# Stacked low-rank product, turned queries, reused conversion buffers and another cost model for the order of the lead, in a one-core attention and mixer kernel

## Chip, cores and metric

The kernel runs on one core of a Trainium2 chip. The metric is the device time of one execution in microseconds (us). Three runs of the kernel before took 1488.79, 1486.19 and 1491.61 us, median 1488.79.

## The reference

Everything is float32. Eight batches (B), eight heads of 64, 576 positions (S), d_model 512.

```python
def sm_attn(qq, kk, vv):
    s = scale * np.matmul(qq, kk.transpose(0, 1, 3, 2))
    s = s - np.max(s, axis=-1, keepdims=True)
    a = np.exp(s)
    a = a / (np.sum(a, axis=-1, keepdims=True) + 1e-09)
    return np.matmul(a, vv)
p_packed = sm_attn(p, k, v)                # p: 32 packed queries per head
x = sm_attn(q, p_packed, p_packed)         # then heads side by side: [B, S, 512]

xk = mu_k * x + (1.0 - mu_k) * x_prev      # x_prev: x one position earlier
xr = mu_r * x + (1.0 - mu_r) * x_prev
k = np.maximum(xk @ w_k, 0.0)              # 512 -> 1024
x = sigmoid(xr @ w_r) * (k * k @ w_v)      # 1024 -> 512

h = x.transpose(0, 2, 1) @ U @ V           # over positions, rank 32
u = x + h.transpose(0, 2, 1)
out = u + np.maximum(u @ w_ch1, 0.0) @ w_ch2   # 512 -> 2048 -> 512
```

## The kernel before

**Parts.** The work falls into three stretches that follow each other on TensorE (PE).

- *The lead* does attention units 0 to 7. A unit is two batches and two heads; there are 16. `attention_steps` transposes K, P, the exponentials and Q with PE (`plan.transpose`, a matmul with the identity, tile `psat`), copies each result out of PSUM, and writes the unit's output `xo` to the DRAM tensor `x_d`. Units 0 to 7 are "plain" (`NPLAIN`), on four buffer sets; units 8 to 15 have a second form of the last softmax, all on buffer set A0.
- *Phase 1* walks 12 chunks of 384 rows (`chunks`, index `n`): mix with the previous position (`mix`), the sigmoid branch (`r_block`, `psr`), the hidden layer (`k_block`, `psk`), its output (`v_block`, `psv`), the product of both to the DRAM tensor `x2_d` (`x2_out`), and the low-rank sum over positions (`xu_block`, `psu`) to `xu_d`. Units 8 to 15 lie between its chunks 2 to 5.
- *Phase 2* has nine blocks `q` of four row tiles T (36 tiles of 128 rows). For each T, `load_u` reads the rows back, `h_block` multiplies by V and adds (`psh`), `t_block` transposes, `operands` makes the seven combinations of a Strassen step, and the loop over `f` (8 steps) does `product` (`psc`, 128x256) and `c2_block` (`psc`, 128x512) with the converted weights.

Float32 products are three float32r matmuls of a high and a low part (`split`: `hi` is a copy, `lo` a difference). The weights come as float64; `Cast.run` turns them into float32 with ACT and DVE operations on staging tiles (`cv.st`, three of 4 KB a row; `cv.tp`, tags "a" and "m", two each of 2 KB). From chunk 2 on, `casts` does V and the 32 tiles of `w_ch1` and `w_ch2` as background work, five a chunk, taking one tile of each weight in turn; `make_ws` builds the Strassen weights from `w_ch1` in chunks 10 and 11 and stores them in `ws_d`, from where GpSimd's queue fetches them all through phase 2 (`load_ws`).

**Queries of units 8 to 15.** `load_q` brings a unit's 288 KB with two DMAs, in runs of 64 floats, one unit ahead of their use (`claim`, `early`). Nine PE transposes of 128x128 in three groups, each followed by a copy (ACT or DVE, whichever the scheduler picks), make `qt`.

**The low-rank product.** `make_v` keeps V as a high and a low part, each with a zero half so that two batches share a tile; `load_xu` makes one tile `X` for two batches, the high part of U's product in one half of the partitions and the rest in the other. `h_block` runs two matmuls of 128x512 per T, one per part of V.

**The order.** Nothing is issued as written. `Plan` records every operation with its engine (or a choice of ACT and DVE), its class `cls` (lower goes first; casts and `make_ws` have 3) and what it depends on, and `emit` builds five queues (PE, ACT, DVE, GpSimd, SP) by simulating itself: each engine has a clock, an operation becomes ready at the end of what it needs plus a lag `LAT` between engines (127 ns from DVE to DVE), and takes a modelled duration; DMAs have modelled issue, transfer and landing times. Each queue then runs strictly in that order, SP's DMAs included: an entry that waits holds all behind it.

Of the kernel before, what the change touches and what calls it, by code (L numbers as in the profile page):

```python
# [9 lines left out]
F32 = mybir.dt.float32  # L10
# [90 lines left out]
class Plan:  # L101
# [234 lines left out]
    TICK = 10240.0 / 3.0  # L336

# [3 lines left out]
    def emit(self):  # L341
# [67 lines left out]
        while True:  # L409
# [46 lines left out]
            if op.cost == "dma":  # L456
                clock[e] = t + (60.0 if e == "sp" else 1000.0)
                dge = max(dge, t + 60.0) + 500.0
                wire = max(wire, dge + 700.0) + dur
                op.fin = wire + 1700.0  # L460
            else:
# [9 lines left out]
                clock[e] = t + dur  # L471
# [6 lines left out]
def packed_attention_moe_mixer_kernel(  # L478
# [98 lines left out]
    class Bufs:  # L577
# [24 lines left out]
        def tile_in(self, tag):  # L602
            return plan.tile(self.big_p, [P, 1152], F32, "big", parts=(0, 1, 2, 3), name=tag)
# [17 lines left out]
        def load_q(self, u, after=()):  # L621
# [3 lines left out]
            t = self.qin[u]  # L625
            for b2 in range(2):
# [21 lines left out]
    def attention_steps(A, u, u_next):  # L648
# [69 lines left out]
        for c in range(3):  # L718
            yield
            ps = ps_att()  # L720
            for t in range(3):
                i = 3 * c + t
                plan.transpose(ps[:, t * P:(t + 1) * P], qin[:, i * P:(i + 1) * P], ident)
            n = 3 if c < 2 or not plain else 2
            w = 8 if plain else NI
            plan.copy(
                qt[:, 0:w * P].rearrange("p (b i c) -> p i b c", b=2, i=w)[:, 3 * c:3 * c + n],
                ps[:, 0:n * P].rearrange("p (i c b) -> p i b c", i=n, b=2))
            if c == 2 and plain:
# [194 lines left out]
    es_w1, es_att, es_x, es_st = ExitStack(), ExitStack(), ExitStack(), ExitStack()  # L924
# [7 lines left out]
    cv = Cast(es_att, "right")  # L932
# [221 lines left out]
    vx_p, st_p, u_p, wb_p, w2r_p, tr_p = rpools = [Pool(bufs=n) for n in (1, 5, 4, 11, 1, 3)]  # L1154

    def open_r():
        es_att.close()
        for n, pl in zip("vx st2 u wb w2r tr".split(), rpools):
# [12 lines left out]
    c2_tags = [(home[t], t) for t in ["wk2_1", "wk3_1"] + [f"wv{m}" for m in range(MK)]]  # L1171
    c2_tags += [(w2r_p, "c2_0"), (w2r_p, "c2_1"), (xs_p, "xs")]
# [17 lines left out]
    def make_v():  # L1190
        vst = plan.tile(vx_p, [P, 2, NI, 2, 64], F32R, "vst", parts=(0, 1))
        vst_.append(vst)
        for c in range(2):
# [3 lines left out]
            for i0, i1 in ((0, 5), (5, NI)):  # L1197
                s = plan.tile(st_p, [P, 512], F32, "s", name="s_v")
                sv = s[:, 0:(i1 - i0) * 64].rearrange("p (i b c) -> p i b c", b=2, c=32)
# [367 lines left out]
```

## Time and profile before

The profiled execution took 1491.34 us; its span, from the first to the last instruction, is 1489.6 us, with 1.7 us around it. It is 2.55 us above the median of the three runs.

| what | in the profiled execution |
|---|---|
| span | 1489.6 us, 25587 instructions |
| PE, matmuls | 1461.4 us busy, 98% |
| DVE | 980.2 us, 66% |
| ACT | 728.3 us, 49% |
| GpSimd | 270.3 us, 18% |
| mean granted PE clock | 0.983 of 2.4 GHz |
| DMA | 292.42 MB, 196 GB/s over the span |

An engine's busy time is the sum of its instructions' spans. Matmuls overlap in the records (each is shown from its start to its modelled end), so the time that a run of matmuls really takes is read from the chain of waits or from start to start. "PEclk" is the granted clock, 1.00 for 2.4 GHz and 0.50 for 1.2 GHz; a value between them is a mean of a stretch that had both.

### The profile page before, as it was taken

Reading aid. Unit: us, or ns where it says so; the run is one execution under the profiler, and the core shown is the slowest. Engines: PE = TensorE matmul, PEld = TensorE weight load, DVE = VectorE, ACT = ScalarE, POOL = GpSimd, SP = SyncE. Lnnn points to the kernel's source line nnn. Section 1 sums busy time; section 2 is a strip of 40 time slices with the busy share of each in tenths; the row PEclk is TensorE's granted clock in tenths of the full one; section 3 lists DMA queues with packets and bytes.
Section 4 is the critical chain, followed back from the end, with each engine's and each line's share of the span. In section 5 each row is a group of like instructions: output and inputs, shape, how many; then the busy total and the mean of one; then the engine's idle time right before and its main releaser. Section 6 shows DMA issues by size and latency. Waiting matters only on the chain.

```text
span 1489.6 us, 25587 instructions
## 1 busy us (share of the span) xinstructions
PE 1461.4 (98%) x9208; PEld 1277.7 (86%) x9208; DVE 980.2 (66%) x2143; ACT 728.3 (49%) x1534; POOL 270.3 (18%) x522
## 2 busy tenths in 40 slices
PE   6999999999999999999999999999999999999998
PEld 5667888888888888889899999899999999999997
DVE  6677877788888888786855464545555555554533
ACT  5567656666666666676533233323333332333332
POOL 0000000000000000001333333333333333333331
PEclk9689999999999999999999999999999999999999
DMA  8863335654655446666988888888888878878763
GB/s 233 234 175 121 114 101 137 205 182 136 186 179 156 141 141 218 207 226 191 314 228 237 211 208 245 198 244 229 231 212 229 213 201 239 213 216 222 206 176 99
DMA packets 213708, 292.42 MB, mean 196 GB/s; under 512 B 70224, under 2 KB 105360, under 8 KB 213584
## 3 DMA queue, kind: packets, MB, share of 16 engines
q1 hardware_dynamic: 141008, 158.65, 34.7%
q0 software_dynamic: 72576, 132.15, 34.0%
q8 instruction: 74, 1.21, 0.3%
q14 instruction: 50, 0.41, 0.1%
HBM read 229.84 MB, written 60.89 MB: 195 GB/s over the span
## 4 chain that ended last, share of the span: by engine, by line
PE 92%; DMA 3%; DVE 2%; SPq 1%; ACT 1%; issue 1%; DVEq 0%
PE psc L197 50%; PE psk L197 13%; PE psv L197 12%; PE psr L197 7%; PE psat L197 5%; PE psat L209 3%; SPq L319 1%; PE psh L197 1%; PE psu L197 1%; DMA kin<-in_k_dram 1%; DMA s<-w_d 1%; DMA qin<-in_q_dram 0%; DMA x_d<-xo 0%; DMA prs<-x_d 0%; DVE ob L254 0%
## 5 line engine op out<-in xcount | busy, mean ns | idle before, releaser
L197 PE MATMUL psc<-w,hid 128*128 128x512 f32 x1728 | 420.7, 391 | 0.2 <-ACT xu L288 0.2
L197 PEld LDWEIGHTS psc<-ob,wb 128*128 128x128 f32 x3024 | 386.4, 191 | 15.1 <-ACT tmp L288 0.8
L197 PE MATMUL psc<-ob,wb 128*128 128x256 f32 x3024 | 391.1, 282 | 0.4 <-ACT tmp L288 0.4
L319 POOL DMA_DIRECT2D wb<-ws_d x504 | 267.3, 530 | 565.5 <-PE psc L197 436.9
L197 PEld LDWEIGHTS psc<-w,hid 128*128 128x128 f32 x1728 | 314.9, 188 | 60.7 <-DVE hid L273 0.7
L233 ACT ACTIVATE hid<-tmp 128x256 fp32r<-128x256 f32 x216 | 131.6, 676 | 229.8 <-DVE tmp L254 229.8
L197 PE MATMUL psk<-xk,wk 128*128 128x384 f32 x1056 | 208.4, 340 | 1.3 <-ACT sq L233 0.8
L197 PE MATMUL psv<-wv,kk 128*128 128x512 f32 x783 | 202.0, 395 | 0.0
L197 PEld LDWEIGHTS psk<-xk,wk 128*128 128x128 f32 x1056 | 184.6, 188 | 10.6 <-issue 1.5
L197 PEld LDWEIGHTS psv<-wv,kk 128*128 128x128 f32 x783 | 144.2, 188 | 28.3 <-issue 0.8
L273 DVE SCALAR_TENSOR_TENSOR hid<-tmp,hid 128x256 fp32r<-128x256 f32 x216 | 126.5, 631 | 49.8 <-ACT hid L233 48.3
L254 DVE TENSOR_TENSOR tmp<-tmp,psc 128x256 f32<-128x256 f32 x288 | 113.1, 410 | 64.4 <-PE psc L197 64.1
L273 DVE SCALAR_TENSOR_TENSOR hid<-psc,hid 128x256 fp32r<-128x256 f32 x72 | 45.3, 629 | 166.5 <-ACT hid L233 166.5
L233 ACT ACTIVATE hid<-psc 128x256 fp32r<-128x256 f32 x72 | 45.9, 637 | 147.9 <-PE psc L197 147.5
L197 PE MATMUL psr<-wr,xr 128*128 128x512 f32 x414 | 112.3, 404 | 0.1
L311 POOL MEMSET x<- 128x8 f32 x4 | 0.5, 113 | 538.4 <-DVE m L270 538.1
L197 PEld LDWEIGHTS psr<-wr,xr 128*128 128x128 f32 x414 | 75.8, 190 | 18.4 <-issue 3.2
L288 ACT ACTIVATE tmp<-psc 128x256 f32<-128x256 f32 x144 | 56.5, 392 | 54.1 <-PE psc L197 53.5
L233 ACT ACTIVATE sq<-psk 128x384 f32<-128x384 f32 x96 | 46.5, 490 | 66.0 <-PE psk L197 63.6
L254 DVE TENSOR_TENSOR kk<-sq,kk 128x384 fp32r<-128x384 f32 x87 | 47.8, 552 | 32.0 <-ACT kk L288 31.8
L270 DVE SCALAR_TENSOR_TENSOR m<-x,mu_t,m 128x384 f32<-128x384 f32 x88 | 51.6, 610 | 0.9 <-ACT m L233 0.9
L233 ACT ACTIVATE m<-x,om_t 128x384 f32<-128x384 f32 x88 | 50.8, 607 | 2.5 <-DVE xr L254 1.8
(176 smaller groups left out, 1645.9 us busy)
## 6 DMA issues: line engine op xcount, KB each, us to landing
wb<-ws_d POOLq DMA_DIRECT2D x504, 256.0 KB, 3.7
st<-in_moe_w_ch_dram SPq DMA_DIRECT2D x32, 512.0 KB, 5.3
ws_d<-wb SPq DMA_DIRECT2D x56, 256.0 KB, 3.0
qin<-in_q_dram SPq DMA_DIRECT2D x32, 288.0 KB, 5.7
x_d<-xo SPq DMA_DIRECT2D x16, 576.0 KB, 3.4
x_d<-x SPq DMA_DIRECT2D x36, 256.0 KB, 2.2
u<-x_d SPq DMA_DIRECT2D x36, 256.0 KB, 5.2
out_dram<-u SPq DMA_DIRECT2D x36, 256.0 KB, 3.2
```

The costliest lines, as they stand in the source:

```text
L197: self.nc.tensor.matmul(o, l, r, start=start, stop=stop, **k)
L209: self.nc.tensor.transpose(out.get(), in_.get(), ident.get())
L233: self.nc.scalar.activation(o, in_.get(), func, **k)
L254: return self.elem(engs, lambda e, o, x, y: e.tensor_tensor(out=o, in0=x, in1=y, op=op), out, [a, b], self.TT, cls)
L270: ("dve",), lambda e, o, x, y, z: e.scalar_tensor_tensor(out=o, in0=x, scalar=z, in1=y, op0=op0, op1=op1), out, [a, b, s], {"dve": (1.042, ...
L273: ("dve",), lambda e, o, x, y: e.scalar_tensor_tensor(out=o, in0=x, scalar=s, in1=y, op0=op0, op1=op1), out, [a, b], self.TT, cls)
L288: self.nc.scalar.activation(o, i, AF.Copy)
L311: (self.nc.gpsimd if eng == "pool" else self.nc.vector).memset(o, 0.0)
L319: (self.nc.sync if eng == "sp" else self.nc.gpsimd).dma_start(out=o, in_=i)
```

## The change

Six things change.

1. **Turned queries.** For units 8 to 15 the nine PE transposes and their three copies go. `load_q` now brings Q with eight DMAs of 32 partitions in runs of 32 floats, arranged so that two 32x32-block transposes on DVE (`plan.turn`, 128x576 each) make `qt`.
2. **Stacked low-rank product.** V is kept as 12 slots of 64 columns, high part in two of the four 32-partition groups and low part in the other two, and `load_xu` makes one tile per batch (`X0`, `X1`) with the matching stack of four. One matmul then holds all four products for two row groups of one batch. A tile T is now two half tiles of one batch (`halves_of`), apart from the ninth of each batch pair, which still takes two matmuls. `load_u` and the output store use two DMAs of 64 rows for such a T.
3. **Buffers.** The staging pools of `Cast` stay open to the end (`es_cv`). In phase 2 the three `cv.st` tiles hold converted `w_ch2` tiles, and `cv.tp` holds `u` tiles; the pools `u` and `w2r` go, and `st2` has 6 buffers instead of 5.
4. **When conversions happen.** All of `w_ch1` is converted ahead of `w_ch2`; the phase-2 pools open after chunk 6, and `make_ws` runs two pairs a chunk in chunks 7 to 10 instead of four in chunks 10 and 11.
5. **Loads in the first block of phase 2.** `load_w2` and the `u` loads of the next block are tied to the step before (`after=(step,)`).
6. **The scheduler's model.** Below 150 us of modelled time (`AHEAD`) an operation of ACT or DVE that depends on one of the same engine is ready 100 or 83 ns before that one's end, not after a lag, and the engine's clock moves on that much earlier. From 500 us of modelled time (`CHUNKS`) DMAs have slower modelled figures. No instruction changes by this, only the order and the choice of ACT or DVE.

```diff
+    AHEAD = 150000.0
+    CHUNKS = 500000.0
+    OVER = {"act": 100.0, "dve": 83.0}
+    LEAD = (60.0, 500.0, 1.0, 1700.0)
+    LOADED = (300.0, 100.0, 1.19, 3000.0)
...
-                return max([p.fin + self.lag(p.eng, e) for p in op.preds], default=0.0)
+                return max([p.fin + (-self.OVER[e] if p.eng == e and e in self.OVER and p.fin < self.AHEAD
+                                     else self.lag(p.eng, e)) for p in op.preds], default=0.0)
...
-                clock[e] = t + dur
+                clock[e] = t + (max(dur - self.OVER.get(e, 0.0), 0.0) if t < self.AHEAD else dur)
...
+            if u >= NPLAIN:
+                for b2 in range(2):
+                    for h in range(2):
+                        src = q[2 * bp + b2, 2 * j + h].rearrange("(r t) (e s) -> e r t s", t=2 * NI, e=2)
+                        for e in range(2):
+                            g = 2 * h + e
+                            plan.dma(t.at(2 * g + b2)[g * 32:(g + 1) * 32, b2 * S:(b2 + 1) * S]
+                                     .rearrange("p (t s) -> p t s", s=32), src[e], after=after)
+                return
...
-        for c in range(3):
+        for c in range(3 if plain else 0):
...
+        if not plain:
+            yield
+            for b2 in range(2):
+                r = slice(b2 * S, (b2 + 1) * S)
+                plan.turn(qt[:, r].rearrange("p (i r e) -> p e i r", i=NI, e=2), qin[:, r])
...
-    vx_p, st_p, u_p, wb_p, w2r_p, tr_p = rpools = [Pool(bufs=n) for n in (1, 5, 4, 11, 1, 3)]
+    vx_p, st_p, wb_p, tr_p = rpools = [Pool(bufs=n) for n in (1, 6, 11, 3)]
...
+    c2_tags = [(cv.st, "st")] * 3
+    c2_tags += [(home[t], t) for t in ["wk2_1", "wk3_1"] + [f"wv{m}" for m in range(MK)]]
...
+        for b2 in range(2):
+            xa = plan.tile(st_p, [P, 512], F32, "s", parts=(0, 1, 2, 3), name="xa")
+            xb = plan.tile(st_p, [P, 512], F32, "s", parts=(0, 1, 2, 3), name="xb")
+            for g in range(4):
+                for a, t in ((0, xa), (1, xb)):
+                    r = a * 64 + b2 * NP
+                    plan.dma(t.at(g)[g * 32:(g + 1) * 32, :], xu_d[b][r:r + NP, :])
+            plan.tt(xa, xa, xb, add)
+            X = plan.tile(vx_p, [P, 512], F32R, f"X{b2}")
...
-        for a in range(2):
-            plan.mm(ps, vst_[0].at(a)[:, a, i].rearrange("p b c -> p (b c)"), xt[b], start=(a == 0), stop=(a == 1))
+        if t < NI - 1:
+            k2 = t % 4
+            plan.mm(ps, vst_[0][:, 2 * k2:2 * k2 + 2].rearrange("p e c -> p (e c)"), xt[b, t // 4],
+                    start=True, stop=True)
+        else:
+            for b2 in range(2):
+                plan.mm(ps, vst_[0][:, NI - 1 + 2 * b2:NI + 1 + 2 * b2].rearrange("p e c -> p (e c)"), xt[b, b2],
+                        start=(b2 == 0), stop=(b2 == 1))
...
-            if n == NCAST:
-                opened_r = plan.open(rpools, A0.pools + cv.pools, open_r)
-        if n > NCAST:
+        if n == FIRST_WS - 1:
+            opened_r = plan.open(rpools, A0.pools, open_r)
+        if FIRST_WS <= n < FIRST_WS + 4:
             plan.cls = 3
-            for f in range(NF // 2):
-                make_ws((n - NCAST - 1) * (NF // 2) + f)
+            for f in range(2):
+                make_ws(2 * (n - FIRST_WS) + f)
...
-                        load_w2(m)
+                        load_w2(m, (step,) if f else ())
```

`FIRST_WS` is 7 and `NCAST` stays 9. Three places show what the scheduler makes of it.

PE in phase 1 where unit 13 stands, before: three groups of three transposes of `qin` lie between the sigmoid branch's matmuls.

```order
L197 MATMUL psr<-wr_200,xr 128x512 x3
L209 MATMUL psat<-ident,qin 128x128 x3
L197 MATMUL psr<-wr_201,xr 128x512 x2
L209 MATMUL psat<-ident,qin 128x128 x3
L197 MATMUL psr<-wr_201,xr 128x512
L197 MATMUL psr<-wr_202,xr 128x512
L209 MATMUL psat<-ident,qin 128x128 x3
L197 MATMUL psr<-wr_202,xr 128x512
```

Now PE has none there, and DVE has two turns per unit, a low half of the hidden layer (`kk`) between them (the same unit).

```order
L254 TENSOR_TENSOR th<-qt,th 128x576
L215 STREAM_TRANSPOSE qt<-qin 128x2x288
L254 TENSOR_TENSOR kk<-sq,kk 128x384
L215 STREAM_TRANSPOSE qt<-qin 128x2x288
L254 TENSOR_TENSOR xr<-m,xr 128x384
```

So the work moved from PE, and from the copies behind it, to DVE's queue; SP's queue has the unit's Q as eight entries in a row where it had two.

PE in phase 2, a step of block 1, before: two matmuls of `psh` per T between the products.

```order
L197 MATMUL psc_9281<-ob,wb 128x256 x6
L197 MATMUL psh<-X,vst 128x512 x2
L197 MATMUL psc_9390<-ob,wb 128x256 x6
```

Now one, at a later step of the same block.

```order
L197 MATMUL psc_9352<-ob,wb 128x256 x6
L197 MATMUL psh<-X_9376,vst 128x512
L197 MATMUL psc_9472<-ob,wb 128x256 x6
```

Over the program `psh` has 72 matmuls before and 40 now; the ninth T of a batch pair keeps two.

PE in the lead, units 0 and 1 (`a_150` are unit 0's exponentials), before:

```order
L209 MATMUL psat<-ident,qin 128x128 x9
L209 MATMUL psat<-ident,kin 128x128 x8
L209 MATMUL psat<-ident,kin 64x128 x2
L209 MATMUL psat<-ident,pbd 128x128
L209 MATMUL psat<-ident,a_150 128x128 x5
L197 MATMUL psat<-kh,pT 32x256 x8
L197 MATMUL psat<-vin,at 32x64 x20
```

Now:

```order
L209 MATMUL psat<-ident,qin 128x128 x9
L209 MATMUL psat<-ident,a_150 128x128 x4
L209 MATMUL psat<-ident,kin 128x128 x4
L209 MATMUL psat<-ident,a_150 128x128
L209 MATMUL psat<-ident,kin 128x128 x4
L209 MATMUL psat<-ident,kin 64x128 x2
L209 MATMUL psat<-ident,pbd 128x128
L197 MATMUL psat<-kh,pT 32x256 x8
L197 MATMUL psat<-vin,at 32x64 x20
```

The same matmuls stand there, with unit 0's ahead of unit 1's; the order differs like this all through the lead, while SP's first 36 rows are the same and later ones change places by a few.

## Rows read from the trace of the kernel before

**Rows 1.** Page, part 1: busy time of each engine and its share.

```profile
PE 1461.4 (98%) x9208; PEld 1277.7 (86%) x9208; DVE 980.2 (66%) x2143; ACT 728.3 (49%) x1534; POOL 270.3 (18%) x522
```

**Rows 2.** Windows: stretch, length, busy us of each engine, PEclk, DMA share, GB/s.

```profile
0.00:60.00 60.00, 45.99 (x403) 34.91 (x404) 39.99 (x108) 31.56 (x89) 1.32 (x11) 0.80 0.84 234
60.00:146.00 86.00, 79.30 (x655) 56.24 (x654) 62.86 (x153) 59.28 (x158) 0.00 (x0) 0.86 0.54 160
...
220.00:510.00 290.00, 288.12 (x1984) 244.36 (x1983) 240.72 (x536) 198.35 (x427) 0.11 (x1) 1.00 0.55 166
...
706.00:728.00 22.00, 21.43 (x128) 18.41 (x127) 20.00 (x39) 13.53 (x28) 6.89 (x13) 1.00 0.95 294
728.00:1480.00 752.00, 752.00 (x4689) 679.87 (x4688) 401.65 (x835) 250.25 (x478) 254.44 (x480) 1.00 0.81 217
```

**Rows 3.** Page, part 4: the chain that ended last, by engine.

```profile
PE 92%; DMA 3%; DVE 2%; SPq 1%; ACT 1%; issue 1%; DVEq 0%
```

**Rows 4.** Chain in order of time, 424 to 432 us: start, us, what.

```profile
426.53 0.33 PE psat L209 x3
426.86 0.47 PE psr L197 x2
427.33 0.33 PE psat L209 x3
...
428.13 0.33 PE psat L209 x3
```

**Rows 5.** Chain in order of time, 745 to 755 us, in phase 2.

```profile
752.04 0.47 PE psh L197 x2
```

**Rows 6.** Groups by form: busy us, mean ns, idle before; first row 220 to 510.

```profile
L209 PE MATMUL psat<-ident,qin 128*128 128x128 f32 x72 | 11.6, 272 | 0.0
...
L197 PE MATMUL psh<-X,vst 128*128 128x512 f32 x72 | 23.0, 396 | 0.0
```

**Rows 7.** Groups by form, 220 to 510 us: turns and copies of qt.

```profile
L288 ACT ACTIVATE qt<-psat 128x384 f32<-128x384 f32 x15 | 7.3, 491 | 4.4 <-PE psat L209 4.2
L215 DVE STREAM_TRANSPOSE qt<-a 128x576 f32<-128x576 f32 x8 | 6.2, 772 | 0.0
L291 DVE COPY qt<-psat 128x384 f32<-128x384 f32 x9 | 5.0, 555 | 4.2 <-PE psat L209 4.2
```

**Rows 8.** Groups by form, whole span: what load_xu does.

```profile
L254 DVE TENSOR_TENSOR xa<-xa,xb 128x512 f32<-128x512 f32 x4 | 2.7, 682 | 0.0
L288 ACT ACTIVATE X<-xa 128x512 fp32r<-128x512 f32 x4 | 2.5, 633 | 7.3 <-PE psh L197 6.9 <-DVE xa L254 0.4
```

**Rows 9.** Timeline of SP, 388 to 432 us: start, us, DMAs issued.

```profile
391.56 3.02 SPq L319 DMA_DIRECT2D qin<-in_q_dram  x2
...
425.82 1.44 SPq L319 DMA_DIRECT2D qin<-in_q_dram  x2
```

**Rows 10.** Page, part 6: DMA issues, KB each, us to landing.

```profile
qin<-in_q_dram SPq DMA_DIRECT2D x32, 288.0 KB, 5.7
...
u<-x_d SPq DMA_DIRECT2D x36, 256.0 KB, 5.2
```

**Rows 11.** Timeline of PE, 695 to 745 us: idle before in brackets.

```profile
725.63 0.98 PE L197 MATMUL psc<-ob,wb 128*128 128x256 f32 x6 [0.41 <-ACT tmp L288]
...
727.24 2.81 PE L197 MATMUL psc<-w,hid 128*128 128x512 f32 x11 [0.16 <-ACT xu L288]
```

**Rows 12.** What PE waited for, whole span: us, times, longest.

```profile
PE psat L209 <- DMA kin<-in_k_dram: 8.7, 5, 3.6
...
PE psu L197 <- DVE xs L291: 1.0, 2, 0.5
```

**Rows 13.** Timeline of DVE, 68 to 70 us.

```profile
68.56 0.41 DVE L264 TENSOR_SCALAR m<-a 128x512 int32<-128x512 int32 x1
68.88 0.42 DVE L277 TENSOR_REDUCE st<-psat 128x1 f32<-128x256 f32 x1
```

**Rows 14.** Timeline of DVE, 700 to 706 us.

```profile
703.19 0.68 DVE L254 TENSOR_TENSOR sums<-ut 128x512 f32<-128x512 f32 x1
703.91 0.69 DVE L254 TENSOR_TENSOR sums<-ut,sums 128x512 f32<-128x512 f32 x1
```

More of the change, by code (lines that the diff above doesn't have):

```diff
@@ L456, in emit @@
             if op.cost == "dma":
[L457 to L460, printed above, removed]
+                issue, gap, share, land = self.LEAD if t < self.CHUNKS else self.LOADED
+                clock[e] = t + (issue if e == "sp" else 1000.0)
+                dge = max(dge, t + issue) + gap
+                wire = max(wire, dge + 700.0) + dur * share
+                op.fin = wire + land
             else:
@@ L602, in tile_in @@
         def tile_in(self, tag):
-            return plan.tile(self.big_p, [P, 1152], F32, "big", parts=(0, 1, 2, 3), name=tag)
+            return plan.tile(self.big_p, [P, 1152], F32, "big", parts=tuple(range(8)), name=tag)
         def load_k(self, u, after=()):
@@ L1190, in make_v @@
     def make_v():
-        vst = plan.tile(vx_p, [P, 2, NI, 2, 64], F32R, "vst", parts=(0, 1))
+        vst = plan.tile(vx_p, [P, 12, 64], F32R, "vst")
         vst_.append(vst)
+        plan.zero(vst[:, NI:NI + 2].bitcast(F32))
         for c in range(2):
@@ new lines, in halves_of, with load_u @@
+    def halves_of(T):
+        b, t = divmod(T, NI)
+        if t == NI - 1:
+            return b, [(slice(0, P), t, slice(0, P))]
+        b2, k2 = divmod(t, 4)
+        return b, [(slice(e * 64, (e + 1) * 64), 2 * k2 + e, slice(b2 * 64, (b2 + 1) * 64)) for e in range(2)]
+    def load_u(T, after=()):
+        b, hs = halves_of(T)
+        pl, tag = (((cv.tp, "a"), (cv.tp, "m")) * 2 + ((r_p, "r"),) * 3 + ((x2_p, "x2"),) * 3)[T % 10]
+        u_t[T] = plan.tile(pl, [P, DM], F32, tag, name="u", parts=(0, 1))
+        for n, (to, i, rows) in enumerate(hs):
+            t = u_t[T].at(n) if len(hs) > 1 else u_t[T]
+            plan.dma(t[to], x2_d[b].at(i)[rows, i * DM:(i + 1) * DM], after=after)
@@ L1360, in c2_block @@
                 dst = out[2 * b:2 * b + 2].rearrange("b (p i) f -> (b p) i f", i=NI)
-                plan.dma(dst[:, i, :], u)
+                for to, i, rows in hs:
+                    plan.dma(dst[rows, i, :], u[to])
     casts = []
@@ L1373, in packed_attention_moe_mixer_kernel @@
         casts.append((slice(0, P), w_ch1[:, m * P:(m + 1) * P], 512, put1))
+    for m in range(MC):
         def put2(w, m=m):
@@ L1463, in packed_attention_moe_mixer_kernel @@
             prep0 = [f for T in range(4) for f in (lambda T=T: h_block(T), lambda T=T: t_block(T))]
-        if n == NCAST + 2:
+        if n == len(chunks) - 1:
             operands(0)
-            for m in range(2):
+            for m in range(3):
                 load_w2(m)
@@ L1479, in packed_attention_moe_mixer_kernel @@
             T0 = 4 * q + 4
-            for T in range(T0, T0 + 4):
-                load_u(T)
+            if q > 0:
+                for T in range(T0, T0 + 4):
+                    load_u(T)
             hs = [[lambda T=T: h_block(T)] for T in range(T0, T0 + 4)]
```

70 lines of the change are left out of this document (28 added, 42 removed).

## The prediction

> **What bounds the kernel now.** I read the busy shares first. PE is busy 98% of the span, no other engine over 66% [rows 1]. Since records of matmuls overlap, that alone proves little, so the chain of waits comes second: 92% of the span is PE [rows 3]. Third, the windows by stretch, because the parts of the change lie in different ones [rows 2]. From 220 to 510 us, where units 8 to 15 lie, PE idles 1.9 of 290 us at the full clock, with DVE at 241 us and ACT at 198. From 728 to 1480 it never idles, and DVE has half its time free. Only the first 146 us look otherwise: there PE idles 14.0 + 6.7 = 20.7 us and the granted clock is 0.80 and 0.86, so part of it runs at 1.2 GHz. From 146 us on, then, a matmul taken away is time taken away, unless what replaces it makes PE wait; in the lead a moved operation can be worth anything from a loss to a gain.
>
> **The queries (phase 1).** Removed: 24 groups of three PE transposes. A record says 272 ns for one [rows 6], but in the chain three take 0.33 us among matmuls that follow without a pause, and each group there shows the same [rows 4]. 24 x 0.33 = **7.9 us**. All of it is on the path, as PE has no idle before them [rows 6].
>
> Behind them go 24 copies, 15 on ACT (7.3 us) and 9 on DVE (5.0 us). Added on DVE: 16 turns of 576 elements. The kernel has turns of that size, at 772 ns [rows 7]: 12.4 us. DVE so gains 7.4 us in this stretch, 241 to 248 of 282 us, 88% instead of 83%. I cost that at nothing: PE hides it, and the flexible copies can go to ACT, which loses 7.3 us. If that cover goes, the low halves of the hidden layer come late; PE now waits 1.0 us for DVE's input to the low-rank sum there [rows 12], the first to grow.
>
> A unit's Q is eight DMAs instead of two on SP. The nearest rows are the two issues of Q, 1.44 to 3.02 us together [rows 9], 0.7 us each at the cheaper; eight then take some 6 us, estimated from that, and the V loads queued behind them start 4 us later. Landing is 5.7 us now [rows 10]; twice as many pieces bound it at 11.4. Loads of one unit were issued at 391.56 and used at 426.53 [rows 9, 4]: 35 us ahead, against at most 6 + 11.4 = 17. Cost nothing.
>
> **The low-rank product.** Of 72 matmuls 40 are left (four T of 36 keep two). Two took 0.47 us in the chain [rows 5]: 32 x 0.235 = **7.5 us**, 28 of them in phase 2, where PE never idles, and four at the end of phase 1. Added are, per batch pair, one more sum, one more high part and one more low part (about 0.68 + 0.63 + 0.69 us, from [rows 8] and the half-height low part as now), four times, 8 us on engines with hundreds free [rows 2]. The extra DMAs (about 100 on SP in phase 2) stand in a queue that mostly waits. At the very end a tile leaves in two pieces, and the last store may issue one DMA later: +0.3 us by the cheaper issues, between 0 and 0.7.
>
> **The handover to phase 2.** Before, PE idles 0.6 us here [rows 2, 11], and matmuls stand apart near those two waits. Eight Strassen builds move out of chunks 10 and 11, so DVE (20.0 of 22 us busy [rows 2]) has less to do: a gain of 0 to 1.5 us. Against it, `u` tiles 2 and 3 now take the buffers of the last conversion, which the schedule leaves until late. DVE's addition waits for a load of 5.2 us [rows 10], with the last hidden layers queued behind. Their consumers on PE run about two blocks later (a block of nine such matmuls is 9 x 0.235 = 2.1 us), 4 us, which covers it; uncovered it costs up to 3 us. I take -0.5, bounds -1.5 to +3.
>
> **The lead.** Only the order changes. In the first 60 us the loads set the pace (DMA at 0.84 of its time, [rows 2]) and SP's order there is the same, so I expect nothing of it. Of the next 86 us, 6.7 are idle and, with a clock of 0.86, 24 us run at half speed (86 x 0.14 x 2), so a perfect order could give back at most 6.7 + 12 us. Is the new model better? Independent DVE operations do overlap: one at 68.56 lasts 0.41 us, the next starts at 68.88, 0.09 before that end [rows 13]. The old model did not know this. But one that needs the other's result does not: from 703.19 plus 0.68 to 703.91 it starts 0.04 after the end [rows 14]. Before, the model waited 127 ns there, 0.09 too much; now it starts 83 ns early, 0.12 too soon. So it is right for one kind of pair and as wrong as before, the other way round, for the other. I take **-2 us**, bounds -10 (about half the ceiling) and +7 (idle time doubled).
>
> The Trainium skill, page "VectorE: DVE Perf Modes", section "The DRAIN you can't avoid", says that the next operation does not start until the pipe of the one before is empty. By that rule the overlap would not exist and the old model would be the right one, so the lead's term would be a loss. The trace disagrees for independent operations [rows 13] and agrees for dependent ones [rows 14].
>
> **Sum.** -7.9 - 7.5 + 0.3 - 0.5 - 2 = -17.6. From 1491.3, the profiled execution, that is 1473.7. The median of the runs lies 2.55 lower, so I forecast **1471 us** for the median. What a measurement can tell from no change is 0.3%, 4.5 us.
>
> **Rivals.**
>
> *The lead gets worse.* The model counts chains of dependent operations on one engine too short, 0.12 us a link, so PE's fixed order places what follows too early, and each softmax has half a dozen links. With the upper bound, +7 instead of -2: 1480. For: [rows 14]. Against: the overlap of independent operations is real, and the old model was off by nearly as much per link. 17%.
>
> *The lead gets much better.* A denser order raises the clock earlier. -10 instead of -2: 1463. For: half speed in 24 us. Against: loads come first until about 60 us, and PE waited 8.7 us for K alone [rows 12], which no order on PE mends. 15%.
>
> *The queries do not do what they say.* The path through 220 to 510 is not PE but what runs beside it, and PE's freed 7.9 us turn into waits for DVE: 1479. For: DVE at 88%, and its turns stand between low halves. Against: 1.9 us of idle in 290. 7%.
>
> *Both the first and the third:* 1471 + 9 + 7.9 = 1488, no change. 4%.
>
> *Slower: queries late at the head of DVE's queue.* A late Q once held only PE's transposes. Now a turn that waits for its DMA holds everything on DVE, the low halves PE needs among it. It decides once a turn stands over 4 us (PE's two blocks of slack) before its landing. To undo -17.6 and lose 4.5 more, each of eight units has to stall PE by 2.8 us, that is, hold DVE for some 7; with 3.5 us a unit, 28 us, it is 1471 + 28 = 1499. For: eight issues, smaller pieces. Against: 35 us of lead over 17 [rows 9, 10]. 3%.
>
> The Trainium skill, page "DMA: Bandwidth & Descriptors", section "Specifications", wants pieces of at least 512 bytes for line rate, and the new ones are 128; Q is below it already, at 256. What twice the pieces would cost is in the 11.4 us above.
>
> **How the numbers follow.** The forecast has 54%. Its own range: lead and handover as above, halves of their bounds, 1465 to 1477. To hold 8 in 10 the range has to reach both lead rivals and the rival of the queries: 1463 at the low end less the handover's last 1 us and the scatter of medians (the runs before spread over 5.4 us, so 2 us), **1460**; 1480 at the high end and the handover's 3 us, **1483**. Left out are the case of no change, the slower one and the far tails. Faster by over 4.5 us: 54 + 17 + 15 + 7 = **93%**; within it **4%**; slower **3%**.
>
> **What would show it.** In the profile after: no PE transpose of `qin` between 220 and 510, 16 turns near 0.77 us; 40 `psh` matmuls near 0.235 us in the chain; the stretch of units 8 to 15 some 8 us shorter; phase 2 from its first product to the end about 6.6 us (28 x 0.235) shorter; PE's idle from 146 to 1480 us still under 6 us; the lead's end, 146 us before, within -10 and +7 of that. It is wrong if DVE or DMA rows on `qt`, `kk` or `xs` appear among PE's waits with more than a few us, if the handover shows more than 3 us of waiting, or if the first 146 us move by more than the bounds.

## The result, and the profile after

The changed kernel takes **1470.26 us**, the median of six runs (1469.05 to 1474.18). The kernel before, run beside it on the same chip, takes 1489.26 us (six runs, 1486.19 to 1492.54). The ratio is 0.9874, 95% interval 0.9855 to 0.9893: 1.3% faster. The forecast was 1471, the range 1460 to 1483. Below, that agreement is taken apart, because its terms were wrong in opposite directions.

The profiled execution of the changed kernel took 1471.11 us and spans 1469.3. Its page and the windows with the bounds of [rows 2] (start and end, length, busy us of each engine with its instructions, granted clock of PE, DMA share, GB/s):

```profile
PE 1435.3 (98%) x9104; PEld 1254.8 (85%) x9104; DVE 987.4 (67%) x2142; ACT 713.9 (49%) x1522; POOL 269.4 (18%) x519
...
PE 90%; DVE 3%; DMA 3%; ACT 1%; SPq 1%; issue 1%; DVEq 0%; ACTq 0%
```

```profile
0.00:60.00 60.00, 42.39 (x476) 30.27 (x476) 45.07 (x123) 37.42 (x106) 1.32 (x11) 1.00 0.90 240
60.00:146.00 86.00, 79.50 (x630) 58.88 (x623) 65.23 (x153) 57.05 (x146) 0.00 (x0) 0.90 0.58 175
...
220.00:510.00 290.00, 286.38 (x1936) 241.41 (x1936) 242.32 (x529) 191.10 (x416) 0.49 (x2) 1.00 0.54 158
...
692.00:712.00 20.00, 20.00 (x126) 17.94 (x125) 16.76 (x34) 10.19 (x22) 6.87 (x13) 1.00 0.79 223
712.00:728.00 16.00, 16.00 (x103) 14.52 (x102) 9.30 (x19) 6.75 (x15) 5.77 (x11) 1.00 1.23 318
```

Three things are to be seen against [rows 1 to 3]. PE still bounds the kernel, with 26 us less of it. In the first 60 us PE ran 476 matmuls instead of 403 and its granted clock is 1.00 instead of 0.80, so in this execution it did not fall from 2.4 to 1.2 GHz there. And from 220 to 510 PE now idles 3.6 us, where it idled 1.9. The handover, which began at 692 here, has no idle at all, where [rows 11] had 0.4 and 0.2.

The parts that were removed or added, by form and in the chain (a group: busy us, mean ns; a chain piece: start, us, what), show what [rows 5 to 7] led one to expect:

```profile
L197 PE MATMUL psh<-X,vst 128*128 128x512 f32 x40 | 15.3, 398 | 0.0
L215 DVE STREAM_TRANSPOSE qt<-qin 128x576 f32<-128x576 f32 x16 | 12.3, 768 | 0.0
```

```profile
746.34 0.23 PE psh L197
```

Sixteen turns of 768 ns stand where 772 was taken, 40 low-rank matmuls are left, and a single one takes 0.23 us in the chain.

To say where the time went I cut both executions at the same pieces of PE's work, read from the starts of its matmuls. All times are of the profiled executions.

```
piece of the work                                      before    after   difference
start to the 192nd key product (psk)                    198.8    189.9     -8.9
192nd to 800th key product (the attention stage)        350.2    345.1     -5.1
800th key product to the first product of phase 2       159.0    158.7     -0.3
first to last product of phase 2 (psc)                  777.1    769.0     -8.1
last product to the end of the span                       4.5      6.6     +2.1
sum                                                    1489.6   1469.3    -20.3
```

The forecast of the span was -17.6, as -2 for the lead, -7.9 for the attention stage, -0.5 at the handover, -7.5 for the low-rank product and +0.3 for the tail. So in these two executions the lead gave 6.9 us more than I took, the attention stage 2.8 less, and the tail cost 1.8 more. Part of the lead's difference is luck, as experiment 1 shows.

### The profile page after: what moved, and what is told of

Its sections match the earlier page's. It is cut to its first block, busy times and chain, and to the rows that moved or that the text cites. A ratio compares the mean times of both kernels' runs of the same rounds, so it can differ in the third digit from the quotient of the medians.

```text
span 1469.3 us, 25583 instructions
## 1 busy us (share of the span) xinstructions
PE 1435.3 (98%) x9104; PEld 1254.8 (85%) x9104; DVE 987.4 (67%) x2142; ACT 713.9 (49%) x1522; POOL 269.4 (18%) x519
## 4 chain that ended last, share of the span: by engine, by line
PE 90%; DVE 3%; DMA 3%; ACT 1%; SPq 1%; issue 1%; DVEq 0%; ACTq 0%
PE psc L197 51%; PE psv L197 12%; PE psk L197 12%; PE psr L197 6%; PE psat L197 4%; PE psat L209 2%; SPq L319 1%; DMA st<-in_moe_w_k_dram 1%; PE psu L197 1%; DMA w_d<-m 1%; PE psh L197 1%; DMA kin<-in_k_dram 0%; ACT a L233 0%; DMA st<-in_moe_w_ch_dram 0%; DVE a L264 0%
## 5 line engine op out<-in xcount | busy, mean ns | idle before, releaser
L197 PEld LDWEIGHTS psc<-ob,wb 128*128 128x128 f32 x3024 | 387.1, 191 | 13.3
L197 PE MATMUL psk<-xk,wk 128*128 128x384 f32 x1056 | 205.2, 339 | 0.1
```

The costliest lines, as they stand in the source:

```text
L197: self.nc.tensor.matmul(o, l, r, start=start, stop=stop, **k)
```

## The experiments

Every kernel was timed beside the kernel before on its own chip, so percentages are compared through their ratios. Between two of them one can tell about 0.26%, 4 us.

**1. The model of the lead, alone and undone.** First the kernel before with the new model for operations of VectorE and ScalarE and nothing else, then the changed kernel without it:

```diff
+    AHEAD = 150000.0
+    OVER = {"act": 100.0, "dve": 83.0}
```

```diff
-    AHEAD = 150000.0
+    AHEAD = 0.0
```

> The kernel before with one part of the change: ACT and DVE operations overlap in the scheduler's model below 150 us. PE's order in the lead is then that of the changed kernel, row for row, and nothing else is meant to differ. Theory A (the order shortens the lead by the 8 to 9 us by which the two traces differ there): 1480 to 1482 us against 1489, the 96th psk matmul near 156 us instead of 164, and half speed of PE's clock in the lead well under the 48 us of before. Theory B (my forecast's size, -2 us, the rest of the 8 being the luck of one profiled execution): 1486 to 1488. Theory C (the lead was worth nothing): 1489.

> The changed kernel with that part alone taken back (overlap below 0 us of modelled time), so PE's lead has the order of the kernel before. Theory A: 1478 to 1479 us, 8 above the changed kernel, with the 96th psk matmul back near 164 us. Theory B: 1472 to 1473. Theory C: 1470.

The model alone: 1481.35 us, ratio 0.9969 (0.9953 to 0.9985), so 0.31% or 4.6 us faster than before. The model undone: 1477.51, ratio 0.9933 (0.9912 to 0.9953), 0.59% or 8.8 us slower than the changed kernel. PE's order in the lead is the changed kernel's in the first and the old one in the second. The lead term is real, and two to four times what I took.

The profiled executions differ in the first 146 us by their granted clock (windows of model alone, then of model undone; columns as above):

```profile
0.00:146.00 146.00, 120.59 (x1125) 90.85 (x1126) 114.74 (x286) 98.63 (x262) 1.31 (x11) 0.98 0.70 202
```

```profile
0.00:146.00 146.00, 122.69 (x1067) 89.33 (x1068) 103.48 (x261) 92.17 (x250) 1.31 (x11) 0.88 0.69 194
```

PE's busy time in the first is 2.1 us less, and yet it has 58 matmuls more behind it: more of that time is at 2.4 GHz. Over the kernels of this study that have one of the two orders (experiment 2 has a third, and in three of the new ones eight of the first 1100 matmuls change places) the clock of these 146 us and the start of the 192nd key product go together:

```
PE's order in the lead   granted clock 0 to 146 us : start of the 192nd key product
old (four executions)    0.84: 198.8  0.85: 198.9  0.88: 196.8  0.94: 189.1
new (nine executions)    0.87: 192.4, 193.7, 193.9  0.89: 190.1  0.91: 189.7  0.92: 191.0
                         0.94: 189.9  0.95: 186.5  0.98: 185.1
```

Two things follow. With one and the same order the lead ends anywhere within 10 us, and goes with the clock of that execution. And at a like clock (0.87 and 0.88, or 0.94) the new order ends between 1 us later and 4 us earlier.

It does not follow that the new order wins by a higher clock. Behind the first 146 us the clock is 1.00 up to the last few us, in the kernel before [rows 2] and in the model alone, so the mean clock of an execution tells of its lead. Over the 17 executions of the kernel before that were timed beside these two kernels that mean is 0.9909, over the 12 of the model alone 0.9905; their spans are 1484.9 and 1479.8 us in the mean. The order wins 5 us, then, with the clock no higher. Nor is PE's idle time smaller: in the first 146 us it is 25.4 us with the model alone and 23.3 with the model undone. In what way the order wins stays open.

The 8.9 us of the table above hold luck besides. The kernel before was profiled in an execution with a mean clock of 0.983, where 58 others of it had 0.987 to 0.997; the changed kernel's was 0.994, the highest of its six (0.985 to 0.994).

**2. Links counted right.** My first rival held that the new model counts dependent operations of one engine 0.12 us too short. Here they start 40 ns after, as the trace has it [rows 14]:

```diff
-                return max([p.fin + (-self.OVER[e] if p.eng == e and e in self.OVER and p.fin < self.AHEAD
+                return max([p.fin + (40.0 if p.eng == e and e in self.OVER and p.fin < self.AHEAD
```

> The changed kernel, but in the planner's model of the lead an operation that needs the one before it on its own engine starts 40 ns after that one's end, as the trace shows it, instead of 83 or 100 ns before. Theory A (PE's order in the lead doesn't hang on these 0.12 us a link): the last key product before the attention stage within 2 us of the changed kernel's 190 us, and the whole within 2.5 us, 1468 to 1473. Rival (links counted too short place PE's work too early and cost waiting): 3 us or more faster, under 1467.3.

1471.36 us, ratio 0.9890 (0.9871 to 0.9909): the same as the changed kernel. The 192nd key product began at 193.6, outside the 2 us of theory A, at a clock of 0.89. In the lead the wrong link costs nothing that can be measured, so what the new model wins there goes with its other half, the overlap of independent operations, which is kept here.

**3. The same model for the whole of phase 1.** The order of the lead stays; the model reaches on to 560 us:

```diff
-    AHEAD = 150000.0
+    AHEAD = 560000.0
```

> The changed kernel, but the planner's model lets operations of VectorE and ScalarE overlap up to 560 us of its time instead of 150, so the order of the attention stage with the feed-forward products changes too; the order up to some 146 us stays. Theory A (the new model's worth lies in the lead, where PE starved and ran at half its clock; behind it PE runs without pause and an order can only win back the 2.8 us of grown waits): the stretch from the 192nd to the 800th key product takes 342 to 347 us, as in the changed kernel (345), and the whole is within 3 us of it, 1467 to 1473. Rival (the model is right for this stage too and removes its waits): that stretch under 342 us and the time under 1467. Against both (dependent operations are counted too short, DVE at 88% now feels it): over 347 us, 1474 or more.

1490.96 us, ratio 1.0031 (1.0016 to 1.0046): the whole gain is gone. The lead is as before (192nd key product at 189.7), but the attention stage takes 361.6 us instead of 345.1. The windows show PE's idle and DVE:

```profile
300.00:400.00 100.00, 93.95 (x645) 76.58 (x645) 89.16 (x191) 62.44 (x138) 0.11 (x1) 0.98 0.64 183
400.00:560.00 160.00, 156.35 (x895) 133.82 (x895) 152.40 (x348) 115.37 (x256) 3.15 (x7) 1.00 0.74 248
```

PE idles 6.1 us in one window and 3.7 in the next, and what it waits for (engine, tile, line, what it waits for: us, times, longest) is led there by VectorE and ScalarE. In the changed kernel the first of these waits is 1.3 us, and the second is not there:

```profile
PE psu L197 <- DVE xs L291: 4.3, 2, 2.2
PE psat L197 <- ACT th L233: 2.8, 3, 1.4
```

So in the lead, where loads and the clock set the pace, a model that is too short did no harm, and here, with DVE busy 89 and 95% of the two windows, the same model did. Two causes stay together here: the short links, and that the planner, thinking DVE faster, put the weight combinations of phase 2 into this stage (the last ends at 562 us instead of 643).

**4. The queries: taken out of the change, and alone.** Taken out, units 8 to 15 have PE transposes, their copies and two loads again:

```diff
-            if u >= NPLAIN:
+            if u >= 99:
...
-        for c in range(3 if plain else 0):
+        for c in range(3):
...
-        if not plain:
-            yield
-            for b2 in range(2):
-                r = slice(b2 * S, (b2 + 1) * S)
-                plan.turn(qt[:, r].rearrange("p (i r e) -> p e i r", i=NI, e=2), qin[:, r])
```

> The changed kernel with the 72 PE transposes, their 24 copies and the two DMAs per unit back for units 8 to 15, everything else as changed. By the forecast's term (7.9 us of PE on the path): 1478. By the traces, in which the stretch from the 192nd to the 800th psk matmul is only 5.2 us shorter because waits grew by 2.8 us: 1475 to 1476. If the queries were worth nothing (rival): 1470.

> The kernel before with the turned queries alone. By the forecast's term 1481.4 us; if waits for SP's eight issues and for DVE take part of it, 1483 to 1485, and the trace shows PE waits on pp, xs or kk in 220 to 510 us that the kernel before has not; if the queries were worth nothing, 1489.

Out of the change: 1478.68 us, ratio 0.9943 (0.9925 to 0.9961), 0.69% slower than the changed kernel. That is 6 to 14 us, with the forecast 7.9 inside. Its attention stage takes 350.0 us; in the changed kernel it is 345.1, and 342.2 to 344.8 in six other kernels of this study that have the turned queries and the buffers, with Q on SP (experiments 2, 7 and 8 and the model undone). So 5 to 8 us of PE are won here.

Alone, put into the kernel before: **1502.73 us**, ratio 1.0107 (1.0085 to 1.0128). The same edit is 1.1% slower without the rest of the change. Its attention stage is as short (345.0 us), but the first to the last product of phase 2 take 793.7 us instead of 777.1. Windows of the handover, and what PE waited for from 680 to 800 us:

```profile
715.00:726.00 11.00, 3.17 (x6) 1.30 (x6) 6.51 (x12) 1.23 (x3) 0.00 (x0) 0.61 1.12 393
726.00:741.00 15.00, 10.28 (x42) 8.44 (x42) 7.71 (x12) 6.47 (x12) 2.64 (x5) 0.83 1.22 311
741.00:760.00 19.00, 18.85 (x110) 16.98 (x111) 16.64 (x34) 10.56 (x21) 6.33 (x12) 0.91 1.03 284
```

```profile
PE psc L197 <- ACT tmp L288: 4.8, 1, 4.8
PE psh L197 <- DVE u L254: 4.3, 3, 2.5
PE psc L197 <- ACT w L288: 3.6, 1, 3.6
```

PE idles 7.8 and 4.7 us, and behind the idle its clock is partly at 1.2 GHz. The chain there names the cause (start, us, what):

```profile
716.34 1.13 DVE ux L215 x2
...
718.42 7.55 DMA s<-w_d
...
725.99 5.76 DMA ut<-uq_d
...
731.82 8.36 DMA s<-w_d
...
740.20 0.63 ACT w L288
```

The first `w_ch2` loads (`s<-w_d`) are issued at 717.9, 13 us after phase 2's first product; before, they were issued from 683, 25 us ahead of it. They are late because all before them is: the last cast is stored at 589.6 us (570.9 before) and the last weight combination is begun at 719.3 (686.0), 20 us after the last key product. And the casts are late in SP's planned order already. Of the 36 stores that `x2_out` makes, three a chunk, 24 stand ahead of the last cast's store in the kernel before, and 27 here: one chunk later. Eight Q loads a unit instead of two take places in SP's modelled queue, and casts move behind them.

**5. That cause, tested.** The turned queries alone again, with the Q loads on GpSimd's queue:

```diff
-                                     .rearrange("p (t s) -> p t s", s=32), src[e], after=after)
+                                     .rearrange("p (t s) -> p t s", s=32), src[e], after=after, eng="pool")
```

> The old kernel with the turned queries alone, as in the run that came out slower than the old kernel, but the eight Q loads of a unit are issued on GpSimd's queue, which has nothing else to do there. In the planned order the casts of the feed-forward weights then stand where they stood in the old kernel again, instead of about one chunk later. Theory A (the turned queries alone were slow since eight Q loads on SP pushed the casts and with them the sixteen weight combinations past the last key product, so that PE starved at the handover and its clock fell): the last combination is built before 695 us, PE idles under 3 us between 690 and 750 us, and the time is 1478 to 1484. Rival (the turns on DVE, not the loads, push the casts): combinations again end after 705 us, 1492 to 1505.

1492.16 us (twelve runs, 1485.39 to 1497.82), ratio 1.0038 (1.0021 to 1.0054), 0.7% better than on SP. The mechanism is as theory A has it: 24 stores ahead of the last cast again, the last combination begun at 678.7 us, and PE idle for 1.7 us in the handover:

```profile
690.00:750.00 60.00, 58.29 (x349) 51.71 (x348) 42.07 (x82) 28.70 (x56) 16.65 (x31) 1.00 0.86 250
```

The time, however, is 8 us above theory A (the profiled execution, at 1485.39, was the fastest of the twelve): the attention stage now takes 352.5 us instead of 345.0. The next run shows a part of why.

**6. The changed kernel with its Q loads on GpSimd's queue.** It was meant to win back the 2.8 us of the attention stage; the edit is the same.

> The changed kernel with the Q loads of units 8 to 15 on GpSimd's queue. Theory A (the 2.8 us by which PE's waits grew in the attention stage come from cast stores that stand behind eight Q issues on SP and hold DVE): 1.5 to 2.8 us shorter, 1467.5 to 1468.8. Rival (another wait takes their place, or the lead's scatter covers it): within 1.5 us of the changed kernel.

1479.30 us, ratio 0.9952 (0.9934 to 0.9969), **slower** by 0.8%, against both theories. The timeline of SP of this run, then of the changed kernel, at the first of these loads (start, us, DMAs issued), and PE's longest wait of this run:

```profile
210.82 3.38 SPq L319 DMA_DIRECT2D kin<-in_k_dram  x4
214.43 3.43 SPq L319 DMA_DIRECT2D x_d<-x  x3
```

```profile
206.82 2.39 SPq L319 DMA_DIRECT2D kin<-in_k_dram  x4
209.31 2.12 SPq L319 DMA_DIRECT2D x_d<-x  x3
```

```profile
219.43 0.63 PE L209 MATMUL psat<-ident,kin 128*128 128x128 f32 x4 [3.70 <-DMA kin<-in_k_dram]
```

GpSimd issues its eight Q loads from 206.7 to 212.2. SP's four K loads here take 3.38 us to issue instead of 2.39 (3.60 in experiment 5 against 2.36 in its partner with Q on SP), and PE waits 3.7 us for K in a place where it did not wait (3.8 in experiment 5).

The slower issue is not the rule: over the 32 K loads issued from 200 to 480 us its median is 0.61 us in all four kernels, and with Q on SP four K loads take up to 3.82 us too (changed kernel, 258 us). What grew throughout is the time from issue to landing: 6.8 us in the median instead of 4.0, and 7.3 instead of 3.9 in experiment 5.

Of what the attention stage lost, 4.8 us here and 7.5 there, this wait is 3.7 and 3.8. The idle time of PE in the whole stage grew by 4.2 and 5.6 us, and behind the wait for K some 3.4 us ran at 1.2 GHz, where the partners had 2.4 throughout. Which of it comes from the queue and which from the order, which the planner made anew, I can't tell. Another 4.0 us of this run's profiled difference lie in the lead, at a clock of 0.87. So what the 2.8 us hang on was not tested cleanly.

**7. The low-rank product and the builds.** Each single matmul issued twice, 32 more in all; and the builds of the weight combinations (`make_ws`) put back to where they stood before, four calls in each of the last two chunks:

```diff
-            plan.mm(ps, vst_[0][:, 2 * k2:2 * k2 + 2].rearrange("p e c -> p (e c)"), xt[b, t // 4],
-                    start=True, stop=True)
+            for _ in range(2):
+                plan.mm(ps, vst_[0][:, 2 * k2:2 * k2 + 2].rearrange("p e c -> p (e c)"), xt[b, t // 4],
+                        start=True, stop=True)
```

```diff
-        if n == FIRST_WS - 1:
+        if n == NCAST:
...
-        if FIRST_WS <= n < FIRST_WS + 4:
+        if n > NCAST:
             plan.cls = 3
-            for f in range(2):
-                make_ws(2 * (n - FIRST_WS) + f)
+            for f in range(NF // 2):
+                make_ws((n - NCAST - 1) * (NF // 2) + f)
```

> The changed kernel, but each single matmul of the low-rank product is issued twice (the second overwrites the first with the same numbers), 32 more in all, as many as the change removed. Theory A (PE is the path there, as the forecast took it): 32 x 0.235 = 7.5 us over the changed kernel, so 1477 to 1479, with all but a few of them after the first product of phase 2. Rival (some of these matmuls lie where PE waits for the additions or the casts anyway): under 5 us, 1471 to 1475.

> The changed kernel with its queries, low-rank product, buffers and model, but the sixteen weight combinations of phase 2 are built where the old kernel built them, four in each of the last two chunks and after all casts, instead of two in each of four chunks from the seventh on. Theory A (the earlier builds are what keeps the turned queries from costing at the handover; the kernel with the turned queries alone ended its builds at 719 us, 20 us after the last key product, and idled 17 us there): PE idles over 5 us between 690 and 750 us and the time is 1477 to 1492. Rival (the early place of the builds is worth little, and the turned queries alone were slow for another reason): within 3 us of the changed kernel, 1468 to 1473.

Twice the matmuls: 1475.42 us, ratio 0.9921 (0.9906 to 0.9936), 0.47% or 7.0 us over the changed kernel. Phase 2 from its first to its last product takes 775.1 us instead of 769.0: 6.1 us for the 27 added matmuls that lie there, 0.226 us each. The time itself lies between the two expected ranges; by the ratio it is near theory A's 7.5 us. PE is the path there, as taken.

Builds late: 1475.32 us, ratio 0.9919 (0.9905 to 0.9934), between the two expectations; but not by theory A's mechanism:

```profile
690.00:750.00 60.00, 59.16 (x362) 52.82 (x361) 40.67 (x82) 28.68 (x56) 17.95 (x35) 1.00 0.99 262
```

PE idles 0.8 us there, not over 5. The last combination is begun at 674.9, still 16 us ahead of the last key product; as I read the kernel, because the builds need only the casts of `w_ch1`, which now come first. Phase 2 takes 769.4 us, as long as in the changed kernel; 3.8 us of the profiled difference of 4.2 lie in the lead, whose order is the same (clock 0.87). Put together with experiments 4 and 5: the handover was clean in the four kernels whose last combination is begun ahead of the last key product (686 us against 704 in the kernel before, 642 against 689 in the changed kernel, 675 against 691 and 679 against 696 in experiments 7 and 5) and broke in the one where it is behind it (719 against 699). At the handover the exact place of the builds is worth little, 0.8 us of idle. The whole is still 0.45% or 6.6 us slower than the changed kernel, more than the 4 us that can be told apart, and what that hangs on is not shown.

**8. The tail.** The second halves of the last tiles leave through GpSimd's queue, and in another kernel through ScalarE's:

```diff
-                for to, i, rows in hs:
-                    plan.dma(dst[rows, i, :], u[to])
+                for n, (to, i, rows) in enumerate(hs):
+                    plan.dma(dst[rows, i, :], u[to], eng="pool" if q == NQ - 1 and n == 1 else "sp")
```

(`eng="act"` in the other.)

> The changed kernel, but in the last group of the output the second half of each tile leaves through GpSimd's queue instead of SP's; the work before is the same. Theory A (the tail grew by about 2 us because seven stores are issued one after the other on SP, some 0.6 us each): 1.0 to 2.0 us shorter, 1468.3 to 1469.5. Rival (the end hangs on the landing of the last store, and GpSimd's issue is no faster): within 0.7 us of the changed kernel.

> The changed kernel, but the second halves of the last output tiles leave through ScalarE's queue, which is empty then; through GpSimd's queue nothing was won, since its stores landed later (up to 4.3 us after the issue instead of 2.4). Theory A (what counts at the end is the chain of issues on one queue): from the last matmul to the end 4.5 to 5.2 us instead of 6.6, and the whole 1.4 to 2.0 us shorter, 1468.3 to 1469. Rival (two queues share what writes the output, and the end hangs on that): 6 us or more from the last matmul to the end.

1472.86 us, ratio 0.9903 (0.9886 to 0.9921), and 1469.25, ratio 0.9882 (0.9861 to 0.9902): neither differs from the changed kernel. The last stores of the changed kernel, then of GpSimd's and ScalarE's (line, queue, count: ns an issue least, median, most; first and last start; below it, us to landing, least, median, most):

```profile
L319 SPq DMA_DIRECT2D out_dram<-u x7: 467/542/597, 1462.0 to 1465.8; - x7
...
DMA to landing us min/median/max: 2.3/2.4/2.5
```

```profile
L319 SPq DMA_DIRECT2D out_dram<-u x4: 466/490/542, 1464.4 to 1466.3; - x4
L319 POOL DMA_DIRECT2D out_dram<-u x3: 534/552/554, 1464.6 to 1465.9; - x3
...
DMA to landing us min/median/max: 3.0/3.7/4.3
```

```profile
L319 SPq DMA_DIRECT2D out_dram<-u x4: 467/488/537, 1463.6 to 1465.5; - x4
L319 ACTq DMA_DIRECT2D out_dram<-u x3: 547/581/696, 1463.6 to 1465.1; - x3
...
DMA to landing us min/median/max: 2.3/2.8/3.8
```

With two queues the last issue ends 1.7 us after the last product begins, instead of 3.6 on one; before it was 1.5. But the stores land later, and from the last product to the end it is 9.0 us by GpSimd and 6.1 by ScalarE, against 6.6. Most of what two queues saved in issuing they gave back in landing. The Trainium skill bears on this: by its page "DMA: Bandwidth & Descriptors", section "Issuing engines are not separate DMA queues", all DMAs run on the same 16 engines, and starting them from several saves only the time of issuing. Both traces agree in that only the issuing got shorter, by 1.9 us, against 1.3 (ScalarE) or 1.8 us (GpSimd) more at the latest landing. What else is in GpSimd's 9.0 us the trace doesn't tell.

No run was faster than the changed kernel beyond what can be told apart.

## Why the prediction was right, and where it was not

**What bounds the kernel:** right. A PE matmul taken away behind 146 us was time taken away, shown by putting the queries' transposes and the low-rank matmuls back.

**The queries, -7.9:** the size of PE's part was right (experiment 4), but "cost nothing" for the rest was not: in the profiled execution 2.8 of the 7.9 us are missing. PE's idle, 3.6 us in this stage instead of 1.9, is 1.7 of them; the other 1.1 I can't assign. I had bounded the eight Q issues and found 35 us of lead over at most 17; that held, as no turn ran late enough to matter. What I did not price was who stands *behind* these issues on SP. The chain of the changed kernel passes through one such place (start, us, what; lines between left out):

```profile
261.94 0.61 SPq L319
...
266.82 0.63 SPq L319
...
269.32 8.81 DMA w_d<-m
...
278.23 0.10 DVE m L264
...
279.59 0.27 DVE pp L270
...
279.91 0.33 PE psat L209
```

Eight issues of Q, about 0.6 us each, fill SP from 261.9 to 267.5; behind them stands the store of a cast, issued at 269.3 and slow to land (8.81 us, where 4.0 is the median of these stores); DVE's next write to that buffer waits for it, and `pp` and PE's transpose wait for DVE, PE for 1.5 us. The prediction had named the V loads behind Q, and not the cast stores. This is read from the chain; that moving Q off SP would cure it was not shown, since experiment 6 brought another wait. Nor does it come in every execution: the two kernels of experiment 8 have the same order in this stage; the one with its last stores on GpSimd's queue has this wait too, 1.5 us, and a stage of 344.6 us, and the one with ScalarE's queue has no such wait, and 343.4.

The rival "the queries do not do what they say" was thus true for a part: of the 7.9 us, 1.1 (stage of 343.4 us) to 2.8 (345.1) did not arrive. The slower rival had DVE's queue held by a late Q; no run shows that. But the same edit *did* turn out slower alone, by a way that I had not thought of: through the planner's order, SP's places and a deadline up to 400 us later. The rest of the change had to be there for the 7.9 us to arrive. The early place of the builds is not what counted in it (experiment 7); that the casts of `w_ch1` come first was not tested alone. My sum priced the parts one by one and could not see that.

**The low-rank product, -7.5, and the handover, -0.5:** right. 27 matmuls cost 6.1 us when put back, 0.226 each where 0.235 was taken, 7.0 us for all 32. From first to last product phase 2 lost 8.1 us with 29 matmuls fewer there, 6.6 us at that price. Of the 1.5 us left, 0.6 is the idle of [rows 11] that is gone; the rest is not assigned. The handover so gave up to 1 us more than taken, within its bounds. The late `u` tiles that I feared left no wait.

**The lead, -2:** wrong by size, and the largest miss. It measured -4.6 alone, 8.8 when undone, and -8.9 in the two profiled executions, which is near the rival "much better" and holds luck. The step that failed is "I expect nothing of it" for the first 60 us. There the loads did set the pace, and yet PE did 73 matmuls more in them; some of that is the full clock of this one execution, but at a like clock, too, the new order had more behind it at 60 us (423, 456 and 457 matmuls in three kernels, at 0.83, 0.84 and 0.86) than the old (396 and 409, at 0.83 and 0.86). What PE computed while waiting for loads was a matter of order. The rival's own reason, that a denser order raises the clock earlier, is not borne out: the order won 5 us with a mean clock no higher (experiment 1). And I weighed the two errors of the model, overlap and links, as if they were equal; experiment 2 shows that the links cost nothing there. By the rule that the prediction took from the Trainium skill's page "VectorE: DVE Perf Modes", section "The DRAIN you can't avoid", the old model would have been the better one and the lead a loss. It measured a gain, as [rows 13] would have it. The section itself has an exception that the prediction left out: an operation that is not held starts earlier.

**The tail, +0.3:** mis-sized, +2.1. I took one issue more, at the cheap end, a few tenths, where three more stand in line. [rows 9] had the right price: 0.7 us a piece when several are issued one behind the other. Seven back to back took 4.29 us (0.61 each), where four before were spread by the sums on DVE, over 2.22:

```profile
1462.02 4.29 SPq L319 DMA_DIRECT2D out_dram<-u  x7
```

**The sum:** 1471 against 1470.26 is closer than the steps deserve, and in part luck: in the profiled executions the lead's surplus of 6.9 us covered what the attention stage (2.8) and the tail (1.8) fell short.

## What to carry to other kernels

A DMA costs more than its landing: it takes a place in a queue, in fact and in a planner's model, and what stands behind it (here casts, then the weight combinations of the next phase) can miss a deadline hundreds of us later. Before adding up the gains of an edit's parts ask which part makes room for which, and try the most promising part alone: here it was 1.1% slower alone and 0.7% faster in place. In a stage where PE waits for loads, the order of the work can be worth more than its idle time shows; here it was worth 5 to 9 us of the first 190, and the same optimistic model cost 16 us in the next stage, where DVE was near full. Compare such stages over many executions: one order scattered there by nearly 9 us.

## What the runs showed of the hardware

- DMAs issued back to back on SP take some 0.6 us each (seven stores in 4.29, eight Q loads in 5.51 at 261.94 us).
- With a unit's Q loads on GpSimd's queue instead of SP's, the K loads on SP from 200 to 480 us landed later, 6.8 and 7.3 us after their issue in the median instead of 4.0 and 3.9, while their issue took 0.61 us either way.
- The last stores land 2.3 to 2.5 us after their issue by one queue, up to 3.8 when ScalarE shares them, and up to 4.3 when GpSimd does.
- With one and the same order of PE's work the granted clock of the first 146 us was 0.87 to 0.98 and the 192nd key product began anywhere from 185.1 to 193.9 us: nearly 9 us of scatter in one stage, more than most edits are worth.
- An idle stretch costs more than itself: with the turned queries alone PE idled 13.3 us between 700 and 800 us, its granted clock was 0.61 to 0.91 from 715 to 760, and phase 2 took 16.6 us longer than in the kernel before.
